# Expert weights through one ring of 22 converted pieces, converted at planned slots, with the staging tiles at another place

## The chip, the cores and the metric

The kernel runs on one core of a Trainium2 chip. The metric is the device time of one execution in microseconds (us). TensorE is called PE, VectorE DVE, ScalarE ACT, GpSimd POOL and SyncE SP. SP issues the DMAs that this text is about.

## The reference

Three layers follow each other: attention with a mask by cluster, a mixture of experts with one expert per token, and a dense layer with a piecewise quadratic activation. The change lies in the second one, which is

```python
for e in range(E):                      # E = 8 experts, N = 1536 tokens, D = 512, F = 1024
    mask = e_idx == e
    h = np.maximum(x[mask] @ w1[e], 0.0)            # w1[e]: 512 x 1024, float32
    ye = h @ w2[e]                                  # w2[e]: 1024 x 512, float32
    out[mask] = gate_w[mask, None] * eom[mask, e, None] * ye
```

All weights of the eight experts are read once: 64 pieces of 512 KB.

## The kernel before, in words

Attention ends with the routing: POOL scatters the tokens' rows (`pay`) to `xs` in DRAM, sorted by expert (L646), and `order()` writes to `regs` which expert comes first, second and so on, largest first. The capacities of the eight places are `CAPS` = 304 to 144 tokens.

Then comes the expert stage, written out by hand slot by slot. A slot is either `l1(r, fc)`, 12 matmuls that make 128 rows of the hidden layer of expert r (hi and lo float16 halves of weights and tokens: L1088, L1089, L1092), or `l2(r, dc)`, 24 matmuls that make 128 rows of its output (L1104 to L1106). After a first stretch of eight `l1` of expert 0, phase r has 12 slots: four `l2` of expert r and eight `l1` of expert r + 1. PE's results go to PSUM (a ring of 7 banks, `ps`) and leave it through ACT (`hT` hi half, L1094) and DVE (`hT` lo half, L1095), or for `l2` through DVE and ACT (L1111 to L1114). `Pipe` emits these steps one slot later. "Urgent" ones come first in a step.

The weights arrive as float32 by SP's DMAs into six staging tiles (`stg`), and each piece is converted into two float16 halves: the hi half by ACT (L1010), the lo half by DVE (L1011); every fourth piece takes two ACT steps (L1006, L1007) and POOL (L1008) instead. The halves go to `wp`, where a whole expert's w1 (`w1h`, `w1l`) and w2 (`w2h`, `w2l`) are tiles with two buffers each. A piece's conversion is emitted one slot after its load (`lag`), all loads of phase r being, one per slot, the four of w2 of expert r + 1 and then the four of w1 of expert r + 2. The instructions of an engine run in the order in which they are emitted, so a conversion that waits for its DMA holds what was emitted behind it on ACT and DVE. `tokens(r, row)` is a transposing DMA from `xs`, also on SP. A load can start when its staging tile was released by the lo half of the piece six before.

In the first slots of each phase from phase 1 on, `windows()` and `ids()` do small steps on DVE and POOL (`ids` scatters the token numbers, L764). `fetch` and `convert` bring the first weights of the dense layer (`w_in`, L1025, L1033 to L1041) at the end of the expert stage. The dense layer (L1265 and on) starts when the experts are done.

Of the kernel before, what the change touches and what calls it, by code (L numbers as in the profile page):

```python
# [7 lines left out]
F32 = mybir.dt.float32  # L8
# [20 lines left out]
CAPS = (304, 256, 224, 208, 192, 176, 176, 144)  # L29
NWIN = 20  # L30
# [110 lines left out]
def build(tc, q, k, v, centroids, w_gate, w_og, w1, w2, w_in, w_out, out):  # L141
# [860 lines left out]
    n_lo, lag = [0], [1]  # L1002
# [9 lines left out]

    def piece(dst_h, dst_l, src, scale):

        a, b = dst_h.shape[1], dst_h.shape[2]
        t = stg.tile([128, a, b], F32, tag="st", name="stg")
        n_lo[0] += 1
        nc.sync.dma_start(out=t, in_=src)
        pool = n_lo[0] > 4 and n_lo[0] % 8 in (1, 5)
        pipe.add(lag[0], lambda: halves(dst_h, dst_l, t, scale, pool))  # L1020
# [30 lines left out]
    def w1_pieces(r, e):  # L1051
        W[r, 1] = t = [wp.tile([128, KD, F], F16, tag=n, name=n) for n in ("w1h", "w1l")]
        return [lambda f=slice(n * 256, (n + 1) * 256): piece(
            t[0][:, :, f], t[1][:, :, f], w1f[ds(e * DM, DM), f].rearrange("(k p) f -> p k f", p=128), SW1) for n in range(4)]

    def w2_pieces(r, e):
        W[r, 2] = t = [wp.tile([128, KF, DM], F16, tag=n, name=n) for n in ("w2h", "w2l")]
        return [lambda n=n: piece(
            t[0][:, 2 * n:2 * n + 2, :], t[1][:, 2 * n:2 * n + 2, :],
            w2f[ds(e * F + n * 256, 256), :].rearrange("(k p) d -> p k d", p=128), SW2) for n in range(4)]  # L1060
# [18 lines left out]
    def l1(r, fc):  # L1079
# [3 lines left out]
        wh, wl = W[r, 1]  # L1083
        p = ps.tile([128, 512], F32, tag="p", name="hps")
        f = slice(fc * 128, (fc + 1) * 128)
# [11 lines left out]
    def l2(r, dc):  # L1097
        cap, c0 = CAP[r], C0[r]
        wh, wl = W[r, 2]
        p = ps.tile([128, 512], F32, tag="p", name="yps")  # L1100
        d = slice(dc * 128, (dc + 1) * 128)
        h = HT[r]
        for f in range(KF):
            nc.tensor.matmul(out=p[:, 0:cap], lhsT=wh[:, f, d], rhs=h[:, 0, f, :], start=(f == 0), stop=False)  # L1104
            nc.tensor.matmul(out=p[:, 0:cap], lhsT=wh[:, f, d], rhs=h[:, 1, f, :], start=False, stop=False)  # L1105
            nc.tensor.matmul(out=p[:, 0:cap], lhsT=wl[:, f, d], rhs=h[:, 0, f, :], start=False, stop=(f == KF - 1))  # L1106
# [10 lines left out]
    PAT = {0: (0, 1, 3, 5)}  # L1117
# [3 lines left out]
    def expert(r):  # L1121
        if r < E:
            eid[r] = reg(regs[0:1, 0, r:r + 1], [ET.SP], E - 1)
# [37 lines left out]
    expert(0), expert(1)  # L1161
    for n, f in enumerate(w1_pieces(0, eid[0])):
        f()
        pipe.step()
        if n == 1:
            tokens(0, row(0))
    ld_q = w2_pieces(0, eid[0]) + w1_pieces(1, eid[1])
    lag[0] = 3
    for n in range(8):
        ld_q[n]()  # L1170
        if n == 1:
            tokens(1, row(1))
        l1(0, n)
        pipe.step()
    gates(0)
    lag[0] = 1
    wnd, idg = windows(), ids()
    for r in range(E):
        expert(r + 2)
        C0[r] = reg(regs[0:1, 2, r:r + 1], ACTDVE, NTK)  # L1180
        ld_q = (w2_pieces(r + 1, eid[r + 1]) if r + 1 < E else []) + (w1_pieces(r + 2, eid[r + 2]) if r + 2 < E else [])
        if r + 3 == E:
            ld_q += [fetch, fetch, fetch]
        if r + 2 == E:
            ld_q += [convert, lambda: None, lambda: None, lambda: None, convert]
        if r + 1 == E:
            ld_q += [convert]
        a, b = 0, 0
        if r + 1 == E:
            pipe.flush()  # L1190
            for _ in wnd:
                pass
            nw = nc.values_load(nwin[0:1, 0:1], min_val=0, max_val=NWIN, skip_runtime_bounds_check_because="a count of windows")
        if 0 in PAT.get(r, ()):
            pipe.step()
        for n in range(12 if r + 1 < E else KD):
            if ld_q:
                ld_q.pop(0)()
            if n == 2 and r + 2 < E:
                tokens(r + 2, row(r + 2))  # L1200
            if n in PAT.get(r, (2, 5, 8, 11)) or r + 1 == E:
                if b < KD:
                    l2(r, b)
                b += 1
            else:
                l1(r + 1, a)
                a += 1
            if r:
                next(wnd, None)
                if n % 3 == 0:  # L1210
                    next(idg, None)
            pipe.step()
        if r + 1 < E:
            gates(r + 1)
        for f in ld_q:
            f()
            pipe.step()
# [5 lines left out]
    with tc.If(nw > 0):  # L1223
        with tc.For_i(0, nw, 1) as i:
            e = reg(tabs[0:1, 0, ds(i, 1)], [ET.SP], E - 1)
            for f in w1_pieces("w", e) + w2_pieces("w", e):
                f()
                pipe.step()
# [132 lines left out]
```

## Time and profile before

| | us |
|---|---|
| median of three executions | 696.34 |
| the three executions | 688.11, 696.34, 697.7 |
| the profiled execution | 688.69 |
| its span in the profile | 686.9 |
| expert stage, first matmul to last | 271.65 to 429.1 |
| dense layer, first matmul | 432.03 |

The span runs from the first to the last instruction, and 1.8 us of the profiled execution lie around it. The executions lie in two groups, one near 688 (the profiled one is among them) and one near 697. Times in rows count from the start of the span.

### The profile page before, as it was taken

How to read it: one execution, taken by the hardware profiler on the slowest of the kernel's cores; microseconds unless marked ns; L12 is line 12 of the kernel's file. 1: busy time of each engine (PE TensorE's matmuls, PEld its weight loads, DVE VectorE, ACT ScalarE, POOL GpSimd, SP SyncE). 2: the span in 40 equal slices, each digit the busy share in tenths (PEclk: the TensorE clock that was granted, in tenths of full speed). 3: DMA queues.
4: the chain of work that ended last, by engine and by line, in shares of the span. 5: the costliest groups of instructions: out<-in, count | busy, mean ns of one | idle time of the engine just before them, and what ended most of it. 6: DMA issues, size and time to landing. Idle time of an engine off the chain costs nothing. (4 is left out here: it accounts for less than half of the span.)

```text
span 686.9 us, 14212 instructions
## 1 busy us (share of the span) xinstructions
PE 594.0 (86%) x5574; PEld 382.1 (56%) x5574; DVE 453.2 (66%) x881; ACT 379.8 (55%) x605; POOL 323.3 (47%) x274
## 2 busy tenths in 40 slices
PE   1798679797979741999989898899999999999996
PEld 1365546565656541689979897344444444444442
DVE  6898978998897962577667768778877874000000
ACT  5387568796869811886667764366657653010000
POOL 9268547786576831234344312276657653021101
PEclk9999878998999955999999999999999999999998
DMA  8877889549732527999999992323322232011000
GB/s 211 171 169 159 179 215 215 134 92 161 143 107 57 89 64 219 323 321 221 183 236 238 286 331 65 113 72 94 106 79 91 92 99 85 1 63 45 24 24 31
DMA packets 142172, 96.30 MB, mean 140 GB/s; under 512 B 97168, under 2 KB 127888, under 8 KB 142096
## 3 DMA queue, kind: packets, MB, share of 16 engines
q1 hardware_dynamic: 139744, 88.60, 52.6%
q0 software_dynamic: 2352, 6.70, 2.7%
q8 instruction: 47, 0.77, 0.5%
q14 instruction: 29, 0.24, 0.1%
HBM read 59.84 MB, written 12.29 MB: 105 GB/s over the span
## 5 line engine op out<-in xcount | busy, mean ns | idle before, releaser
L486 POOL TENSOR_TENSOR pl<-p,ph 128x768 f16<-128x768 f32 x64 | 114.0, 1800 | 47.2 <-ACT ph L480 24.9
L445 DVE TENSOR_REDUCE mq<-s 128x1 f32<-128x768 f32 x96 | 90.5, 950 | 17.8 <-PE s L440 17.5
L475 ACT ACTIVATE p<-st 128x768 f32<-128x768 f32 x96 | 75.8, 810 | 32.6 <-PE st L471 29.5
L480 ACT ACTIVATE ph<-p 128x768 f16<-128x768 f32 x96 | 77.5, 847 | 0.8
L1280 POOL TENSOR_TENSOR gt<-gx,gt 128x512 f16<-128x512 f32 x48 | 55.6, 1159 | 46.7 <-ACT gt L1279 46.7
L1265 PE MATMUL mps<-x,wih 128*128 128x512 f16 x192 | 72.8, 379 | 2.9 <-PEq L1223 2.9
L508 PE MATMUL pv<-vh,pl 128*128 128x65 f16 x576 | 65.9, 200 | 10.4 <-DVE pl L486 10.3
L1088 PE MATMUL hps<-xt,w1h 128*128 128x176 f16 (+6 forms) x256 | 54.0, 264 | 21.9 <-DMA xt<-xs 16.9
L1290 PE MATMUL ops<-woh,gt 128*128 128x512 f16 x192 | 72.8, 379 | 0.0
L1291 PE MATMUL ops<-wol,gt 128*128 128x512 f16 x192 | 72.8, 379 | 0.0
L1292 PE MATMUL ops<-woh,gt 128*128 128x512 f16 x192 | 72.8, 379 | 0.0
L1266 PE MATMUL mps<-x,wih 128*128 128x512 f16 x192 | 72.8, 379 | 0.0
L1267 PE MATMUL mps<-x,wil 128*128 128x512 f16 x192 | 72.8, 379 | 0.0
L470 PE MATMUL st<-aT 128*128 128x384 f16 x192 | 67.1, 350 | 3.9 <-DVE mq L445 2.6
L471 PE MATMUL st<-q2T,bT 82*128 82x384 f16 x192 | 67.1, 349 | 0.6 <-DMA q2T<-kq 0.6
L506 PE MATMUL pv<-vh,ph 128*128 128x65 f16 x576 | 66.6, 200 | 0.0
L507 PE MATMUL pv<-vl,ph 128*128 128x64 f16 x576 | 66.3, 198 | 0.0
L1104 PE MATMUL yps<-hT,w2h 128*128 128x176 f16 (+6 forms) x256 | 63.3, 254 | 2.7 <-DVE hT L1095 2.1
L1105 PE MATMUL yps<-hT,w2h 128*128 128x176 f16 (+6 forms) x256 | 63.3, 254 | 0.4 <-DVE hT L1095 0.2
L1106 PE MATMUL yps<-hT,w2l 128*128 128x176 f16 (+6 forms) x256 | 63.3, 254 | 0.0
L440 PE MATMUL s<-bT 80*128 80x384 f16 x192 | 51.6, 367 | 13.0 <-ACT p L475 5.6
L1274 ACT ACTIVATE sq<-cl,c 128x512 f32<-128x512 f32 x48 | 34.6, 722 | 50.2 <-DVE cl L1272 49.6
(220 smaller groups left out, 1435.9 us busy)
## 6 DMA issues: line engine op xcount, KB each, us to landing
stg<-in_moe_w_dram SPq DMA_DIRECT2D x64, 512.0 KB, 6.8
stg<-in_moe_w_in_dram SPq DMA_DIRECT2D x16, 512.0 KB, 3.6
stg<-in_moe_w_out_dram SPq DMA_DIRECT2D x16, 512.0 KB, 3.6
xs<-zrow SPq DMA_DIRECT2D x16, 288.0 KB, 3.8
kqf<-in_k_dram SPq DMA_DIRECT2D x16, 192.0 KB, 3.3
kqf<-in_q_dram SPq DMA_DIRECT2D x16, 192.0 KB, 3.3
vf<-in_v_dram SPq DMA_DIRECT2D x16, 192.0 KB, 3.4
xs<-zrow SPq DMA_DIRECT2D x8, 108.0 KB, 3.7
```

The source lines that it names most:

```text
L445: nc.vector.tensor_reduce(out=mq[:, i, t:t + 1], in_=lg_t.pop((i, t))[:, :, 0:HS], axis=AX.XY, op=ALU.max)
L470: nc.tensor.matmul(out=o, lhsT=aT[i][:, c, 0, :], rhs=aT[i][:, ts, 1, :], start=True, stop=False)
L471: nc.tensor.matmul(out=o, lhsT=bT[i][0:KS2, 0, c, :], rhs=q2T[i][0:KS2, ts, :], start=False, stop=True)
L475: nc.scalar.activation(out=p.rearrange("p (e s) -> p e s", e=2), in_=lg_t.pop(("t", i, c))[:, :, 0:HS], func=AF.Exp, scale=SCALE)
L480: nc.scalar.activation(out=ph_t[i, c], in_=p_t[i, c], func=AF.Copy)
L486: eng.tensor_tensor(out=pl_t[i, c], in0=p_t.pop((i, c)), in1=ph_t[i, c], op=ALU.subtract)
L1265: nc.tensor.matmul(out=p, lhsT=wih[:, kk, :], rhs=x2[:, 0, kk, c], start=(kk == 0), stop=False)
L1266: nc.tensor.matmul(out=p, lhsT=wih[:, kk, :], rhs=x2[:, 1, kk, c], start=False, stop=False)
L1267: nc.tensor.matmul(out=p, lhsT=wil[:, kk, :], rhs=x2[:, 0, kk, c], start=False, stop=(kk == KD - 1))
L1290: nc.tensor.matmul(out=p, lhsT=gt[:, 0, f, c], rhs=woh[:, f, :], start=(f == 0), stop=False)
L1291: nc.tensor.matmul(out=p, lhsT=gt[:, 0, f, c], rhs=wol[:, f, :], start=False, stop=False)
L1292: nc.tensor.matmul(out=p, lhsT=gt[:, 1, f, c], rhs=woh[:, f, :], start=False, stop=(f == KF2 - 1))
```

## The change

Converted weights are no longer held as whole experts. Each piece of 128 x 4 x 256 elements gets its own pair of tiles (`wh`, `wl`) from one ring of 22 (`NWP`), used in the order in which PE needs the pieces. A piece of w2 is now half of the hidden rows and half of the output columns, so an `l2` needs two pieces instead of four, and a row of such a load is 1 KB instead of 2 KB. The slots are listed first (`slots`), with the same patterns as before. A plan (`when`) says ahead of which slot each piece is converted: from an assumed time of arrival (1.75 us a piece, 2.75 us for a transposing DMA, `come`) and an assumed time of each slot (`at`). A load is issued right behind the conversion of the piece six before it. The conversion's ACT steps are now emitted at once, ahead of that slot's matmuls and of the eviction steps of the slot before; the lo half still comes through `Pipe` one step later. `tokens(r + 2)` moves to the first slot of phase r; the three `fetch` move to the middle of phase 5, ahead of the last five weight loads (before, of the last four); the `convert` steps move to slots 6 and 10 of phase 6 and to the first slot of phase 7; `nw` is read one phase earlier. The pools are opened in another order, so that `stg` and `wp` lie behind `hp`, `yp`, `wn` and `xp` in SBUF, over other tiles of the attention.

```diff
-    stg = mes.enter_context(tc.tile_pool(name="stg", bufs=6))
-    wn = mes.enter_context(tc.tile_pool(name="wn", bufs=1))
-    wp = mes.enter_context(tc.tile_pool(name="wp", bufs=2))
-    xp_ = mes.enter_context(tc.tile_pool(name="xp", bufs=2))
     hp = mes.enter_context(tc.tile_pool(name="hp", bufs=2))
     yp = mes.enter_context(tc.tile_pool(name="yp", bufs=3))
+    wn = mes.enter_context(tc.tile_pool(name="wn", bufs=1))
+    xp_ = mes.enter_context(tc.tile_pool(name="xp", bufs=2))
+    stg = mes.enter_context(tc.tile_pool(name="stg", bufs=6))
+    wp = mes.enter_context(tc.tile_pool(name="wp", bufs=NWP))
...
-        pipe.add(lag[0], lambda: halves(dst_h, dst_l, t, scale, pool))
...
+    def load(r, e, z, j):
+
+        t = stg.tile([128, KD, 256], F32, tag="st", name="stg")
+        f, d = j % 2, j // 2
+        src = w1f[ds(e * DM, DM), j * 256:(j + 1) * 256] if z == 1 else w2f[ds(e * F + f * 512, 512), d * 256:(d + 1) * 256]
+        nc.sync.dma_start(out=t, in_=src.rearrange("(k p) f -> p k f", p=128))
+        staged.append((r, z, j, t))
+
+    def conv():
+        r, z, j, t = staged.pop(0)
+        n_lo[0] += 1
+        W[r, z, j] = h, l = [wp.tile([128, KD, 256], F16, tag=n, name=n) for n in ("wh", "wl")]
+        halves(h, l, t, SW1 if z == 1 else SW2, n_lo[0] > 4 and n_lo[0] % 8 in (1, 5))
...
+    when, come = {}, -5.0
+    for k, p in enumerate(pieces):
+        come += 1.75 + (2.75 if p[1:] == (1, 0) else 0.0)
+        n = 0
+        while n < use[p] - 2 and (at[n] < come + 0.5 or k >= NWP and n <= rel[pieces[k - NWP]]):
+            n += 1
+        when.setdefault(n, []).append(p)
...
+    NST = 6
+    for k in range(NST):
+        next_load()
+        if k == 1:
+            tokens(0, row(0))
...
+        for _ in when.get(n, ()):
+            conv()
+            next_load()
+            if n == 0:
+                pipe.step()
+        if first and ph + 2 < E:
+            tokens(ph + 2, row(ph + 2))
+        if (ph, m) == (E - 3, 6):
+            for _ in range(3):
+                fetch()
+        if (ph, m) in conv64:
+            convert()
+        (l1 if z == 1 else l2)(r, i)
```

The order on SP at the start of the expert stage, before. `DMASW` semaphores are those of the scatters to `xs`:

```order
L1046 TENSOR_LOAD regs [waits DVE_49]
L1046 TENSOR_LOAD regs
L1018 ISA
L1018 DMA stg<-in_moe_w_dram 128x4x256 [waits DMASW6_49,DMASW7_49,DMASW5_49,DMAHW0_49,DMASW4_49,DMAHW1_49,DMASW3_49,DMAHW2_49,DMASW2_49,DMAHW3_49,DMASW1_49,DMAHW4_49,DMASW0_49,DMAHW5_49,DVE_49,DMAHW6_49,PE_49,DMAHW7_49,Activation_49,Pool_49]
L1018 ISA
L1018 DMA stg<-in_moe_w_dram 128x4x256
L1046 TENSOR_LOAD regs
L1065 ISA
L1065 DMA_TRANSPOSE xt<-xs 128x4x304
```

The same place after:

```order
L1038 TENSOR_LOAD regs [waits DVE_49]
L1050 ISA
L1050 DMA stg<-in_moe_w_dram 128x4x256 [waits DMAHW2_49,DMAHW3_49,DMAHW1_49,DMAHW4_49,DMAHW0_49,DMAHW5_49,DVE_49,DMAHW6_49,PE_49,DMAHW7_49,Activation_49,Pool_49]
L1050 ISA
L1050 DMA stg<-in_moe_w_dram 128x4x256 [waits DMAHW4_49]
L1038 TENSOR_LOAD regs
L1062 ISA
L1062 DMA_TRANSPOSE xt<-xs 128x4x304 [waits DMAHW5_49,DMASW7_49,DMASW3_49]
L1063 ISA
```

The wait for the scatters moved from the first weight load to the first transposing DMA; the two loads stand ahead of it as before.

The order on ACT around the change from expert 6 to expert 7 and up to the last weights, before (the first `hT` of 128x144 is the first result of expert 7, and `w2h` are the last four pieces):

```order
L1046 TENSOR_LOAD regs
L1094 ACTIVATE hT<-hps 128x144
L1006 ACTIVATE stg<-stg 128x1024
L1007 ACTIVATE w2h<-stg 128x1024
L1113 ISA
L1113 ACTIVATE x_5482<-yps 128x176
L1094 ACTIVATE hT<-hps 128x144
L1010 ACTIVATE w2h<-stg 128x1024 x2
L1094 ACTIVATE hT<-hps 128x144
L1010 ACTIVATE w2h<-stg 128x1024
```

The same place after, from the fourth `hT` of expert 7 on (L1032 and L1033 belong to `convert`; two pieces of expert 7's w2 follow later still, in phase 7):

```order
L1091 ACTIVATE hT<-hps 128x144
L1011 ACTIVATE wh<-stg 128x1024 x2
L1091 ACTIVATE hT<-hps 128x144
L1032 ACTIVATE wih<-cw 128x512
L1033 ACTIVATE cv<-cw 128x512
L1110 ISA
L1110 ACTIVATE x_5482<-yps 128x176
L1091 ACTIVATE hT<-hps 128x144
L1007 ACTIVATE stg<-stg 128x1024
L1008 ACTIVATE wh<-stg 128x1024
L1011 ACTIVATE wh<-stg 128x1024
```

Before, the four conversions of expert 7's w2 stand behind its first, second and third `hT`; after, the first of them (L1007, L1008) stands behind the sixth `hT` of that expert.

## Rows read from the trace of the kernel before

**Rows 1.** The page: span, busy time of each engine, share, instructions.

```profile
span 686.9 us, 14212 instructions
PE 594.0 (86%) x5574; PEld 382.1 (56%) x5574; DVE 453.2 (66%) x881; ACT 379.8 (55%) x605; POOL 323.3 (47%) x274
```

**Rows 2.** PE's timeline: start, length, instruction, idle time before, what ended it.

```profile
271.65 0.41 PE L1088 MATMUL hps<-xt,w1h 128*128 128x304 f16 x1 [16.91 <-DMA xt<-xs]
...
428.89 0.23 PE L1106 MATMUL yps<-hT,w2l 128*128 128x144 f16 x1
432.03 0.38 PE L1265 MATMUL mps<-x,wih 128*128 128x512 f16 x1 [2.92 <-PEq L1223]
```

**Rows 3.** Waits of PE from 262 to 436: total, times, longest.

```profile
PE hps L1088 <- DMA xt<-xs: 16.9, 1, 16.9
PE hps L1088 <- DVE hT L1095: 5.0, 3, 2.2
...
PE yps L1104 <- DVE hT L1095: 2.1, 3, 1.1
PE gp L1074 <- DVE hT L1095: 1.6, 1, 1.6
PE yps L1104 <- ACT hT L1094: 0.6, 1, 0.6
```

**Rows 4.** Stretches of 24 matmuls: length, busy times, PE's clock, DMA share, GB/s.

```profile
352.36:355.76 3.40, 3.40 (x25) 3.17 (x25) 3.40 (x9) 2.38 (x7) 0.00 (x0) 0.56 1.52 137
357.90:359.88 1.98, 1.98 (x27) 1.98 (x26) 1.92 (x4) 1.91 (x3) 1.82 (x2) 1.00 1.08 309
410.88:412.39 1.51, 1.51 (x27) 1.51 (x25) 0.92 (x4) 1.51 (x4) 1.40 (x1) 1.00 0.05 20
416.54:419.28 2.74, 2.74 (x24) 2.63 (x24) 2.74 (x4) 1.04 (x3) 1.16 (x1) 0.54 0.63 185
```

**Rows 5.** ACT's timeline at two conversions that waited for their piece.

```profile
349.01 1.06 ACT L1010 ACTIVATE w1h<-stg 128x1024 f16<-128x1024 f32 x1 [3.48 <-DMA stg<-in_moe_w_dram]
408.71 1.06 ACT L1006 ACTIVATE stg<-stg 128x1024 f32<-128x1024 f32 x1 [3.45 <-DMA stg<-in_moe_w_dram]
```

**Rows 6.** DVE's timeline at the same two places.

```profile
350.33 0.37 DVE L1095 SCALAR_TENSOR_TENSOR hT<-hps,hT 128x208 f16<-128x208 f32 x1 [4.35 <-ACT hT L1094]
350.62 1.21 DVE L1011 SCALAR_TENSOR_TENSOR w1l<-stg,w1h 128x1024 f16<-128x1024 f32 x1
...
411.28 0.31 DVE L1095 SCALAR_TENSOR_TENSOR hT<-hps,hT 128x144 f16<-128x144 f32 x1 [4.63 <-ACT hT L1094]
```

**Rows 7.** Waits of SP from 262 to 436.

```profile
SPq L1018 <- DVE w2l L1011: 17.5, 12, 3.2
SPq L1018 <- POOL w1l L1008: 12.5, 7, 2.5
...
SPq L1018 <- DMA xs<-pay,pos: 3.8, 1, 3.8
```

**Rows 8.** SP's timeline: the first weight loads and the first transposing DMA.

```profile
264.83 1.02 SPq L1018 DMA_DIRECT2D stg<-in_moe_w_dram  x2
266.31 1.82 SPq L1065 DMA_TRANSPOSE xt<-xs  x1
```

**Rows 9.** Line L1018: the last load's start, and from its start to its landing.

```profile
L1018 SPq DMA_DIRECT2D stg<-in_moe_w_dram x1: 372/372/372, 402.5 to 402.5; - x1
...
DMA to landing us min/median/max: 10.1/10.1/10.1
```

**Rows 10.** Stretches as in Rows 4, for the last two columns, DMA share and GB/s.

```profile
310.20:312.20 2.00, 2.00 (x21) 1.61 (x19) 1.89 (x5) 0.75 (x2) 0.00 (x0) 1.00 0.02 5
396.00:405.00 9.00, 9.00 (x123) 8.77 (x121) 7.65 (x12) 7.32 (x16) 2.13 (x1) 1.00 1.09 348
406.00:410.00 4.00, 4.00 (x60) 4.00 (x58) 0.65 (x3) 1.25 (x2) 0.00 (x0) 1.00 1.05 385
324.00:332.00 8.00, 8.00 (x78) 7.22 (x77) 5.68 (x9) 3.64 (x9) 3.91 (x3) 1.00 0.98 154
```

More of the change, by code (lines that the diff above doesn't have):

```diff
@@ L1115, in l2 @@
         pipe.add(1, scaled, True)
-    PAT = {0: (0, 1, 3, 5)}
+    PAT = {0: (0, 1, 3, 5), E - 1: range(KD)}
+    slots = [(1, 0, n, -1) for n in range(KF)]
+    for r in range(E):
+        a = b = 0
+        for n in range(KF + KD if r + 1 < E else KD):
+            if n in PAT.get(r, (2, 5, 8, 11)):
+                slots.append((2, r, b, r))
+                b += 1
+            else:
+                slots.append((1, r + 1, a, r))
+                a += 1
+    at, use, rel = [0.0], {}, {}
+    for n, (z, r, i, _) in enumerate(slots):
+        for j in ([i // 2] if z == 1 else [i // 2 * 2, i // 2 * 2 + 1]):
+            use.setdefault((r, z, j), n)
+            rel[r, z, j] = n
+        at.append(at[-1] + (12 if z == 1 else 24) * CAPS[r] / 2400)
+    pieces = sorted(use, key=lambda k: use[k])
+    when, come = {}, -5.0
[5 more added lines that the diff above has]
+        when.setdefault(n, []).append(p)
     ACTDVE = [ET.Activation, ET.DVE]
@@ L1159, in row @@
         return reg(regs[0:1, 1, r:r + 1], [ET.SP], (E - 1) * NTK)
-    expert(0), expert(1)
-    for n, f in enumerate(w1_pieces(0, eid[0])):
-        f()
-        pipe.step()
[L1165 to L1217, printed above, removed]
@@ new lines, in build, with next_load @@
+    left = list(pieces)
+    def next_load():
+        if left:
+            r, z, j = left.pop(0)
+            if r not in eid:
+                expert(r)
+            load(r, eid[r], z, j)
+    NST = 6
[3 more added lines that the diff above has]
+            tokens(0, row(0))
+    wnd, idg = windows(), ids()
+    phase = -2
+    conv64 = [(E - 2, 6), (E - 2, 10), (E - 1, 0)]
+    for n, (z, r, i, ph) in enumerate(slots):
+        first = ph != phase
+        if first:
+            phase, m = ph, 0
+            if z == 2:
+                pipe.step()
+            if ph >= 0:
+                C0[ph] = reg(regs[0:1, 2, ph:ph + 1], ACTDVE, NTK)
+            if ph == E - 2:
+                nw = nc.values_load(nwin[0:1, 0:1], min_val=0, max_val=NWIN, skip_runtime_bounds_check_because="a count of windows")
+        for _ in when.get(n, ()):
+            conv()
+            next_load()
+            if n == 0:
+                pipe.step()
+        if first and ph + 2 < E:
[6 more added lines that the diff above has]
+        (l1 if z == 1 else l2)(r, i)
+        if z == 1 and i + 1 == KF:
+            gates(r)
+        if ph >= 1:
+            next(wnd, None)
+            if m % 3 == 0:
+                next(idg, None)
+        m += 1
+        pipe.step()
@@ L1225, in build @@
             e = reg(tabs[0:1, 0, ds(i, 1)], [ET.SP], E - 1)
[L1226 to L1228 removed]
+            for z in (1, 2):
+                for j in range(4):
+                    load("w", e, z, j)
+                    pipe.step()
+                    conv()
+                    pipe.step()
             tokens("w", reg(tabs[0:1, 1, ds(i, 1)], [ET.SP], E * NTK - 128))
```

33 lines of the change are left out of this document (10 added, 23 removed).

## The prediction

> **What bounds the kernel now.** The page says that PE is busy for 594.0 of 686.9 us [rows 1]. The dense layer behind the experts runs PE without a break, so a gain has to come from the time up to its first matmul at 432.03. The expert stage takes from 271.65 to 429.1 on PE (the last row's start and length) [rows 2]; the gap of 2.92 behind it is a branch, which stays. I read next what PE waits for in it [rows 3]: first 16.9 us for the first tokens, which is the change of stage; then 8.7 us (5.0 + 2.1 + 1.6) for DVE's `hT`, the step that empties PSUM. DVE is not the cause: its `hT` at 350.33 and 411.28 waited 4.35 and 4.63 for ACT [rows 6], and ACT stood before a conversion whose piece had not landed, 3.48 and 3.45 us [rows 5]. The second one is a piece of w2 of expert 7, which PE first uses in the last phase, some 14 us later (four `l2` of 1.51 [rows 4] ahead of 429.1). So PE is held not by weights that it needs, but by evictions that are queued behind a conversion of weights that it does not need yet. Two of these pauses cost a second time: behind them PE's clock was granted at 0.56 and 0.54 on the mean of the stretch, between the levels of 1.2 and 2.4 GHz, and the same 24 matmuls took 3.40 instead of 1.98 and 2.74 instead of 1.51 [rows 4], together 2.65 us.
>
> The transfers are the second bound, close to the first. The last weight load starts at 402.5 and lands 10.1 later, at 412.6 [rows 9]; DMA engines were idle for two clear us around 311, and in the other stretches of those rows their share is near or over 1 [rows 10].
>
> **The start.** SP's wait of 3.8 us ahead of the first weight load is for the scatters, which read `pay` [rows 7]; the staging tile lay over it. After the change the first load waits for no scatter, and the transposing DMA waits for them, which it has to for its data. The first two loads thus move from 264.83 to about 261.0, and the transposing DMA, now not behind them, from 266.31 [rows 8] to about 264.3 (264.83 less 0.5 for the ten semaphores that SP stepped through). PE starts when it lands. If it takes the same time from its issue, that is 2.0 us; at most the two loads (1.4 us each by the rates below) no longer move ahead of it either, with half of this hidden by its own issue of 1.82: 3.4. Against it, the last scatters now share the DMA engines with two loads; a scatter of 0.29 MB would at most take 0.9 longer (its own time again at 348 GB/s), so that the gain lies between 1.1 and 3.4. I take 2.5, near the upper middle, since the two loads need 2.8 us and have 3.3 of their own ahead of 264.3. The Trainium skill (DMA: Bandwidth & Descriptors, Queues, rings and completion order) says that an engine takes turns between the queues that have work, packet by packet; by it the 0.9 would be paid in full and the term be 1.6. No row here shows two such queues beside each other.
>
> **PE's waits.** A conversion now stands at the slot for which its piece is planned to have landed, and w2 pieces of expert 7 stand behind the sixth `hT` of that expert and later, where before the first stood behind its first `hT`. If pieces land on time, the 8.7 us of waits and the 2.65 of clock go: 11.3. What stays are 0.6 for ACT's `hT` right behind the first expert's `l1` [rows 3], as the slots there are the same, the small pause between slots, and the lower clock at the start. PE alone would then end at 429.1 - 11.3 - 2.5 = 415.3.
>
> **The transfers.** The number of loads, transposing DMAs and `ids` scatters is unchanged. Three things move the last landing: the start, -3.8; the idle time at 311, where SP stood before `tokens`, -2.0 if nothing new idles; and the rows of w2, which halve to 1 KB. Between 396 and 405 w1 and `w_in` moved, 1 KB rows, at 348 GB/s; from 406 to 410 w2, 2 KB rows, at 385 [rows 10]. A piece of 0.524 MB takes 1.51 instead of 1.36 us, over 32 pieces of w2 4.6 us more. The last landing is then 412.6 - 3.8 - 2.0 + 4.6 = 411.4. Behind it come its hi half, 1.06 [rows 5], its lo half, 1.21 [rows 6], the rest of the `l2` that needs it from its middle on, 0.75, and one more `l2`, 1.51 [rows 4], and 0.2 to the end: 416.1. So the transfers would end the stage 0.8 later than PE alone. The slow stretch around 324 to 332 (154 GB/s at a share of 0.98 [rows 10], some 4.5 us lost) is in both kernels. The Trainium skill's rule speaks otherwise here: its table of DMA properties (DMA: Bandwidth & Descriptors, Specifications) puts the smallest transfer for full rate at 512 B, so 1 KB rows would cost nothing and the transfers end at 411.5; the two rates above disagree with it, and the sum goes by the rates.
>
> **Other steps.** ACT, DVE and POOL convert as many elements as before (64 pieces, 15 of them with POOL), and PE's matmuls are the same, so these cost nothing as long as they lie in the evictions' gaps. The conversion's ACT steps now come ahead of the eviction of the slot before, which delays that eviction by 1.06 or 2.1 us; seven PSUM banks cover this, and without them it would be paid at each of the 64. The `convert` steps stay in phase 6 and 7; three DVE steps of 0.7 us each sit beside evictions there, as they did before, and are part of the waits around 416. Reading `nw` earlier only moves a register load. A ring of 22 pieces against 16 gives no wait of its own: the tile that a conversion takes over was last read more than two experts earlier. New waits can come where transposing DMAs, slow stretches and `w_in` fall together with a conversion. Bounds: none, or the 11.3 us of before again. The three old blocks (around 350, 388 and 416) cost 3.8 each; I allow half a block, 1.9, since most conversions are planned several slots ahead of their piece's use, but the transfers have hardly any reserve.
>
> **The sum.** The later of 415.3 and 416.1, plus 1.9, is 418.0, 11.1 earlier than before. The profiled execution took 688.69, so that the same execution would take 677.6. The median of before lies 7.65 above that execution, as two of three lie in a group near 697. What makes the groups I do not know, and a median of three can fall into either, so I add half of it, 3.8: 681.4 us. The 2% that a measurement of this kernel can tell from no change are 13.9 us.
>
> **Rivals.**
> First, everything goes: no new wait, and 1 KB rows as fast as 2 KB. PE alone sets the end, 415.3, and the profiled execution would take 674.9. For it speaks that the conversions are the only thing seen in the way of evictions; against it the two rates. 0.2.
> Second, it doesn't do what it says: the loads stay the bound. A load still waits for the lo half of the piece six before it; SP stood 17.5 and 12.5 us in such waits [rows 7]. Now the conversion is tied to a slot, so a load may be held by PE's progress, where before it followed the landing. If DMA engines idle for 6 us in all by this (a tenth of a us per piece), the end moves to 424, the gain is 5, and the execution takes 683.6. 0.2.
> Third, slower: pieces land later than the plan says (10.1 us from start to landing for the last one [rows 9]), and as the conversion is now emitted ahead of evictions at every slot, each late piece holds ACT. With one block of 3.8 in each of eight phases, 30.4 us come and 13.0 (429.1 to 416.1) go: 706.1. It decides from the seventh block on, where 26.6 reaches 13.0 + 13.9. 0.1, since on the average the plan's rate (eight pieces of 1.75 and 2.75, 16.8 us a phase) is near what the rates give: 12.1 for eight pieces, and a transposing DMA and a share of the slow stretches on top.
>
> **How the numbers follow.** The forecast has 0.5. The low end is the first rival with the better start (674.0), with 2 to 3 us of scatter: 671. The high end is the second rival in the upper group (691.3) with the worse start and some scatter: 694; it leaves out the third rival and little else. Faster by over 2% comes from two thirds of the first rival (0.13), two fifths of the forecast (0.20) and a little of the second (0.02); slower from most of the third (0.08); the rest is within.
>
> **What would show it.** In the changed kernel's profile: first weight load near 261 and first matmul near 269; PE's waits for `hT` in the expert stage under 3 us in all; the clock at 1.00 from soon behind the first matmuls to the end; the last landing near 411; the first matmul of the dense layer near 421. Wrong would be: ACT waiting over 3 us for a piece at several slots, PE's clock at half in the middle of the stage, a share of the DMA engines under 0.5 for several us, or w2 loads at 385 GB/s in spite of their short rows.

## The result and the profile after

The changed kernel takes 701.16 us (median of 20 executions, 695.59 to 706.27) against 694.61 of the kernel before (20 executions): ratio 1.0118, 95% interval 1.0087 to 1.0149. The ratio compares the faster executions of the two kernels, so it is not the quotient of the two medians, which is 1.0094. By the ratio the changed kernel is 8 us slower (6 to 10), within the 2% that count as no change; 681.4 was forecast, and the range ended at 694.

The profiled execution took 703.38, more than the median; the one of the kernel before, 688.69, lies near the low end of its executions (688.11 to 701.40). The two profiles are thus 14.7 us apart, almost twice what the times say, and part of that is scatter. Its page:

```profile
span 701.6 us, 14199 instructions
PE 605.0 (86%) x5574; PEld 385.8 (55%) x5574; DVE 456.0 (65%) x881; ACT 380.3 (54%) x605; POOL 322.1 (46%) x274
```

PE's timeline at the first matmul of the experts, the last one and the first of the dense layer, which answer to [rows 2]:

```profile
273.53 0.41 PE L1085 MATMUL hps<-xt,wh 128*128 128x304 f16 x1 [15.27 <-DVE wl L1012]
...
442.02 0.23 PE L1103 MATMUL yps<-hT,wl 128*128 128x144 f16 x1
444.61 0.38 PE L1282 MATMUL mps<-x,wih 128*128 128x512 f16 x1 [2.36 <-PEq L1237]
```

From the first of them to the third it is 171.08 us; before it was 160.38. So the expert stage is 10.7 of the 14.7 us longer; 1.9 come ahead of it and 2.1 behind it. What comes ahead is not the change: the routing's last step, which everything waits for, is DVE's `CAST` to `regs`, and it came at 257.99 before and at 261.59 here (over all profiles of this text, whose code up to there is the same, it came between 258 and 267):

```profile
261.59 0.17 DVE L687 CAST regs<-rf 1x32 int32<-1x32 f32 x1
```

From its end to PE's first matmul it was 13.5 us before and is 11.8 now. What follows is the stage. PE's waits from 262 to 448, the answer to [rows 3]:

```profile
PE hps L1085 <- DVE wl L1012: 15.3, 1, 15.3
PE hps L1085 <- DMA xt<-xs: 7.6, 2, 4.5
PE yps L1103 <- DVE wl L1012: 4.5, 4, 1.5
PE hps L1086 <- DVE wl L1012: 4.0, 4, 2.0
...
PE yps L1102 <- DVE hT L1092: 1.1, 1, 1.1
PE yps L1101 <- DVE hT L1092: 0.5, 1, 0.5
```

The 15.3 are the change of stage. Of the waits for `hT`, 9.3 in [rows 3], 1.6 are left. In their place stand two that before did not have: 8.5 us in eight waits for a lo half `wl` that DVE has not made yet, and 7.6 in two waits for the tokens of experts 4 and 5. Behind them the clock falls. Stretches of PE alone: length, busy time, clock, DMA share, GB/s:

```profile
359.94:366.77 6.83, 5.03 (x32) 0.50 0.99 297
383.83:387.25 3.42, 3.12 (x22) 0.50 0.90 252
288.26:291.67 3.41, 3.41 (x16) 0.50 0.91 284
sum 13.66, PE 11.55; mean PE 3.85
```

At 0.50 the granted clock is 1.2 GHz, so of 11.55 busy us half, 5.8, is lost by estimate; the first two stretches follow the waits for tokens, the third a wait of 2.0 for `wl`. Together this is 8.5 + 7.6 + 1.6 + 5.8 = 23.5 us, against 9.3 + 2.65 = 11.95 before: 11.5 more, for a stage that grew by 10.7.

The transfers, in stretches with all engines (the last three columns are clock, DMA share and GB/s):

```profile
292.00:296.00 4.00, 3.44 (x26) 2.15 (x24) 1.99 (x3) 2.95 (x6) 0.00 (x0) 1.00 0.04 12
...
369.00:376.00 7.00, 7.00 (x85) 7.00 (x83) 4.09 (x9) 5.57 (x10) 3.69 (x2) 1.00 0.97 45
...
412.00:427.00 15.00, 13.66 (x186) 12.80 (x183) 12.11 (x24) 11.85 (x25) 4.28 (x3) 1.00 1.10 348
```

Three things are to be seen. Weights still move at 348 GB/s in a clear stretch. DMA engines are idle at 292, because SP stands before loads whose staging tile is not free (one wait of 7.0 for a lo half between 287 and 298). Over the stage its waits for lo halves are now 57.9 us:

```profile
SPq L1050 <- DVE wl L1012: 44.3, 22, 7.0
...
SPq L1050 <- POOL wl L1009: 13.6, 10, 2.3
```

Before they were 42.6: the 17.5 and 12.5 of [rows 7], 0.6, and a row that [rows 7] leaves out:

```profile
SPq L1018 <- POOL w2l L1008: 12.0, 6, 4.5
```

And at 369 the engines are busy to 0.97 and move 45 GB/s. In such stretches `ids` scatters are in flight, twelve issued between 311.5 and 375, 8.8 us from issue to landing in the median. The tokens of expert 4 were issued into such a stretch (349 to 353, 59 GB/s), and PE waited for them:

```profile
348.66 6.87 SPq L1065 DMA_TRANSPOSE xt<-xs  x1
```

```profile
361.74 0.32 PE L1085 MATMUL hps<-xt,wh 128*128 128x192 f16 x1 [4.55 <-DMA xt<-xs]
```

They took 12.9 us from issue to landing; the median of such transfers was 6.9 before. They also had less time: they were issued 13.1 us ahead of PE's first use, before 21 (331.31 to 352.36), although they now stand in the first slot of the phase.

### The profile page after: what moved, and what is told of

Same layout as the page of the kernel before. It is cut to its first block, busy times and chain, and to the rows that moved or that the text cites. A ratio compares the mean times of both kernels' runs of the same rounds, so it can differ in the third digit from the quotient of the medians.

```text
span 701.6 us, 14199 instructions
## 1 busy us (share of the span) xinstructions
PE 605.0 (86%) x5574; PEld 385.8 (55%) x5574; DVE 456.0 (65%) x881; ACT 380.3 (54%) x605; POOL 322.1 (46%) x274
## 5 line engine op out<-in xcount | busy, mean ns | idle before, releaser
L1009 POOL TENSOR_TENSOR wl<-stg,wh 128x1024 f16<-128x1024 f32 x15 | 33.2, 2214 | 108.8 <-ACT wh L1008 108.8
L1085 PE MATMUL hps<-xt,wh 128*128 128x176 f16 (+6 forms) x256 | 55.4, 268 | 22.9 <-DVE wl L1012 15.3
L471 PE MATMUL st<-aT 128*128 128x384 f16 x192 | 69.9, 364 | 2.5 <-DVE mq L446 1.5
L472 PE MATMUL st<-q2T,bT 82*128 82x384 f16 x192 | 70.2, 366 | 0.8 <-DMA q2T<-kq 0.8
L1012 DVE SCALAR_TENSOR_TENSOR wl<-stg,wh 128x1024 f16<-128x1024 f32 x49 | 65.3, 1344 | 7.9 <-ACT wh L1011 7.9
L507 PE MATMUL pv<-vh,ph 128*128 128x65 f16 x576 | 68.7, 203 | 0.0
L508 PE MATMUL pv<-vl,ph 128*128 128x64 f16 x576 | 68.3, 201 | 0.0
L1011 ACT ACTIVATE wh<-stg 128x1024 f16<-128x1024 f32 x49 | 51.2, 1057 | 31.0 <-DMA stg<-in_moe_w_dram 30.7
L1103 PE MATMUL yps<-hT,wl 128*128 128x176 f16 (+6 forms) x256 | 63.4, 255 | 4.7 <-DVE wl L1012 4.5
L1102 PE MATMUL yps<-hT,wh 128*128 128x176 f16 (+6 forms) x256 | 63.4, 254 | 1.1 <-DVE hT L1092 1.1
```

The lines of the kernel that those rows point to most:

```text
L471: nc.tensor.matmul(out=o, lhsT=aT[i][:, c, 0, :], rhs=aT[i][:, ts, 1, :], start=True, stop=False)
L472: nc.tensor.matmul(out=o, lhsT=bT[i][0:KS2, 0, c, :], rhs=q2T[i][0:KS2, ts, :], start=False, stop=True)
```

## Experiments

The theories, as the traces suggested them. In the first four runs the first is that tokens come late by their place in SP's queue, the second that six staging tiles hold the loads. Later runs name them A (the 1 KB rows of w2), B (the `ids` scatters' slow stretches), C (loads held by conversions that come late) and D (PE itself waits for lo halves of pieces that have long landed). "Stage" is the time from the first matmul of the experts to the first of the dense layer in the profiled execution; it was 160.4 before and 171.1 after. Ratios are to the kernel before, timed on the same chip, from four to ten executions of each run. A stage is one execution and scatters by some us: with the staging tiles moved the kernel before has 165.0 and is faster all the same. So differences of under 5 us in that column say little.

| run | us | ratio, 95% interval | stage |
|---|---|---|---|
| tokens first | 708.63 | 1.0125, 0.9991 to 1.0259 | 176.0 |
| tokens a phase earlier | 706.27 | 1.0216, 1.0139 to 1.0293 | 174.6 |
| nine staging tiles | 706.33 | 1.0137, 1.0050 to 1.0224 | 170.7 |
| before, staging tiles moved | 694.79 | 0.9936, 0.9880 to 0.9993 | 165.0 |
| before, scatters later | 687.30 | 0.9876, 0.9792 to 0.9960 | 153.9 |
| before, both of these | 686.19 | 0.9853, 0.9807 to 0.9899 | 152.2 |
| before, 1 KB rows | 698.98 | 1.0058, 1.0019 to 1.0097 | 168.0 |
| before, 1 KB rows, scatters later | 686.03 | 0.9877, 0.9773 to 0.9981 | 155.7 |
| after, 2 KB rows | 715.48 | 1.0278, 1.0165 to 1.0391 | 186.6 |
| after, 2 KB rows, scatters later | 703.49 | 1.0114, 1.0010 to 1.0219 | 173.5 |
| after, scatters later | 693.80 | 0.9929, 0.9887 to 0.9972 | 160.6 |
| ... and nine staging tiles | 693.00 | 0.9967, 0.9925 to 1.0010 | 159.1 |
| ... and four slots | 685.99 | 0.9882, 0.9845 to 0.9918 | 155.8 |
| ... and the plan 4 us earlier | 682.81 | 0.9807, 0.9705 to 0.9910 | 149.7 |
| ... and four slots, plan 4 us earlier | 679.82 | 0.9804, 0.9734 to 0.9874 | 152.0 |
| ... and four slots, plan 8 us earlier | 686.10 | 0.9905, 0.9863 to 0.9946 | 155.1 |
| after, four slots | 704.84 | 1.0109, 0.9978 to 1.0240 | 169.2 |
| after, four slots, plan 4 us earlier | 699.59 | 1.0060, 1.0010 to 1.0111 | 171.5 |

**Tokens ahead of the first slot's loads**, in the changed kernel:

```diff
+        if first and ph >= 0 and ph + 2 < E:
+            tokens(ph + 2, row(ph + 2))
         for _ in when.get(n, ()):
             conv()
             next_load()
...
-        if first and ph + 2 < E:
+        if first and ph < 0:
             tokens(ph + 2, row(ph + 2))
```

> The changed kernel, with tokens(r + 2) ahead of the first slot's loads on SP instead of behind them. Theory 1 (the loss is SP's queue: a load that waits for the lo half of the piece six before holds the transposing DMA behind it, and PE waits for late tokens): the two long waits for tokens (7.6 us in all) and the clock behind them go, 8 to 12 us faster than the changed kernel, ratio to the kernel before near 0.998. Theory 2 (the loads are held by the slots of the conversions, DMA engines idle, everything lands late): the waits move from the tokens to the weights, within 4 us of the changed kernel, ratio 1.006 to 1.012.

Measured 1.0125, not the 0.998 of the first theory. The waits moved; PE's, from 272 on (the 16.8 are 15.0 for the change of stage and 1.8):

```profile
PE hps L1085 <- DMA xt<-xs: 16.8, 2, 15.0
PE yps L1103 <- DVE wl L1012: 5.5, 5, 2.0
PE yps L1101 <- ACT hT L1091: 4.2, 1, 4.2
PE hps L1086 <- DVE wl L1012: 4.0, 4, 2.0
PE yps L1101 <- ACT g L1073: 2.5, 1, 2.5
```

**Tokens a whole phase earlier**, into a third tile (the ring has 20 pieces to make room):

```diff
-        if first and ph + 2 < E:
-            tokens(ph + 2, row(ph + 2))
+        if first and ph < 0:
+            tokens(1, row(1))
+        if (ph, m) == (-1, 4):
+            tokens(2, row(2))
+        if first and 0 <= ph < E - 3:
+            tokens(ph + 3, row(ph + 3))
```

> The changed kernel with each expert's tokens issued a whole phase earlier, into a third tile (the ring has 20 pieces for it, which moves no conversion). Theory B in its narrow form (the tokens are late because their DMA is issued late and meets the scatters): the pauses at slots 44 and 56 go, 8 to 10 us, ratio 0.998 to 1.003. If what is short is the transfers' time itself: PE waits for weights at other slots instead, as when the tokens went ahead of one slot's loads, 1.007 to 1.015.

Measured 1.0216, above both forecasts and no better than the changed kernel. No wait for tokens is left, and PE waits for evictions instead:

```profile
PE yps L1103 <- DVE wl L1012: 5.0, 5, 1.4
PE hps L1086 <- DVE wl L1012: 4.0, 4, 2.0
PE yps L1102 <- DVE hT L1092: 3.6, 3, 2.0
PE hps L1085 <- DVE hT L1092: 3.0, 3, 1.6
PE yps L1101 <- ACT g L1073: 2.7, 1, 2.7
```

The place of the tokens alone is thus not the cause: whoever goes first, somebody waits while the scatters run. The first theory falls.

**Nine staging tiles** instead of six, the ring at 20 pieces:

```diff
-NWP = 22
+NWP = 20
-    stg = mes.enter_context(tc.tile_pool(name="stg", bufs=6))
+    stg = mes.enter_context(tc.tile_pool(name="stg", bufs=9))
-    NST = 6
+    NST = 9
```

> The changed kernel with nine staging tiles instead of six, so that a load is issued behind the conversion of the piece nine before (the ring of converted pieces is 20 for the space; the plan is the same with it). Theory 2 (loads are held by the conversions' slots): DMA engines no longer idle between the first two transposing DMAs, and the stage gains 6 to 12 us, ratio 0.995 to 1.003. Theory 1 (SP's queue ahead of the tokens): loads ahead of the tokens wait for the same lo halves, under 3 us, ratio 1.007 to 1.012.

Measured 1.0137: nothing gained. PE still waits 4.6 + 3.9 for `wl` and 9.0 ahead of experts 4 and 5.

**The staging tiles alone**, in the kernel before (`stg` and `wp` behind `hp`, `yp`, `wn` and `xp` in the order of the pools):

```diff
+    hp = mes.enter_context(tc.tile_pool(name="hp", bufs=2))
+    yp = mes.enter_context(tc.tile_pool(name="yp", bufs=3))
+    wn = mes.enter_context(tc.tile_pool(name="wn", bufs=1))
+    xp_ = mes.enter_context(tc.tile_pool(name="xp", bufs=2))
     stg = mes.enter_context(tc.tile_pool(name="stg", bufs=6))
-    wn = mes.enter_context(tc.tile_pool(name="wn", bufs=1))
     wp = mes.enter_context(tc.tile_pool(name="wp", bufs=2))
...
```

> The kernel before, with nothing but the pools opened in the changed kernel's order. If the place of the staging tiles gives the earlier start that was forecast: the first weight load stands about 2.5 us behind regs and not behind the scatters, first matmul 1.5 to 3 us sooner after regs, ratio 0.996 to 0.998. If the loads from the new place are slower or the start is given back by later waits: 1.000 or more.

Measured 0.9936, 4.4 us (0.5 to 8.3). From `regs` to the first matmul it took 11.0 us instead of 13.5. The rest of the 4.4 is in no row: in the profile the stage behind it is longer than before.

**The scatters later**, in the kernel before: `ids` steps in the first half of the dense layer.

```diff
-                if n % 3 == 0:
-                    next(idg, None)
...
-    for _ in idg:
-        pass
...
             if (fc, g) in slots64:
                 convert()
+            next(idg, None)
             pipe.step()
+    for _ in idg:
+        pass
```

> The kernel before, with the scatters of the token numbers (ids, L764) moved from the expert stage into the dense layer. If they make the slow stretches of the transfers (154 GB/s at a share of 0.98 from 324 to 332): these go, DMA has some 10 us less to do, and PE's waits for hT shrink by 3 to 8 us, ratio 0.989 to 0.996. If the stretches have another cause: no change, ratio 0.998 to 1.002.

Measured 0.9876, 8.6 us (3 to 14). From 310 to 400 the transfers move 238 GB/s with the scatters and 269 without (the last columns are clock, DMA share, GB/s):

```profile
310.00:400.00 90.00, 84.46 (x930) 81.45 (x929) 64.76 (x129) 63.37 (x109) 36.23 (x22) 0.98 1.07 238
```

```profile
310.00:400.00 90.00, 89.79 (x980) 85.68 (x979) 71.08 (x137) 69.58 (x119) 21.50 (x10) 1.00 0.87 269
```

The same move in the **changed kernel**:

> The changed kernel with the ids scatters moved behind the expert stage, into the first half of the dense layer. In the kernel before the same move gave 0.9876. Theory A and theory C: it gains what it gave there, 8 to 9 us, and stays about 12 us above the kernel before with the same move, 692 to 694 (ratio 0.995 to 1.0). Theory B: the pauses for tokens of 4.8 and 3.3 us with their half clock (some 12 us) go as well, and the time comes to 680 to 684 (ratio 0.98 to 0.985), level with or below the kernel before with the same move.

Measured 0.9929, about the time that A and C gave. It gains 13 us where the kernel before gains 8.6, but the two intervals are too wide to tell these gains apart, or the two kernels, between which 0.5% remain. No wait for tokens is left within the stage, as B said, although they were issued only 10.6 and 9.4 us ahead of experts 4 and 5; they landed after 6.7 in the median. The waits for `wl` stay at 8.4. So B holds for the tokens, and something else is left.

**The rows of w2.** In the changed kernel, 2 KB rows again; an expert's first `l2` then needs all four pieces:

```diff
+            nc.sync.dma_start(out=t.rearrange("p (a k) f -> p a (k f)", a=2), in_=w2f[ds(e * F + j * 256, 256), :].rearrange("(k p) d -> p k d", p=128))
...
-        for j in ([i // 2] if z == 1 else [i // 2 * 2, i // 2 * 2 + 1]):
+        for j in ([i // 2] if z == 1 else range(4)):
```

> The changed kernel with w2 loaded again in rows of 2 KB, 256 rows by 512 columns a piece, as before; an expert's first l2 then needs all four pieces, as before. Theory A (the rows): the 1 KB rows of w2 are what costs. By the packets of the expert stage, 34,700 of 1 KB at a mean of 61 ns after against 18,900 at 54 and 8,200 of 2 KB at 111 before, they take 11.7 us more of the 16 DMA engines, and the transfers set the end, so the time falls by 8 to 12 us to about 691 (ratio to the kernel before 0.99 to 1.0). Theory B (the ids scatters' slow stretches meet tokens that have no reserve): the time stays within 3 us of the changed kernel's, 698 to 704. Theory C (a load is held until PE has come to the slot of its conversion): also 698 to 704, and the idle stretches of the DMA engines stay.

The same with the scatters later:

> The changed kernel with both: w2 in rows of 2 KB and the ids scatters behind the expert stage. Theory A with the scatters' own price: about 682 (ratio 0.98). If both A and B hold, 674 to 678 (0.97 to 0.976), below the kernel before with the scatters moved. Theory C: 692 to 694, no more than the scatters' own price.

Measured 1.0278 and 1.0114, slower by 1.6 and 1.9% than the same with 1 KB rows. This does not price the rows, since the order of need changed with them; PE's waits up to 445 in the first of the two say so (8.5 in the changed kernel):

```profile
PE hps L1087 <- DVE wl L1012: 13.0, 7, 4.2
PE yps L1104 <- DVE wl L1012: 9.3, 7, 3.1
```

The clean form is the other way round, 1 KB rows in the **kernel before**, with its order kept:

```diff
-            t[0][:, 2 * n:2 * n + 2, :], t[1][:, 2 * n:2 * n + 2, :],
-            w2f[ds(e * F + n * 256, 256), :].rearrange("(k p) d -> p k d", p=128), SW2) for n in range(4)]
+            t[0][:, n % 2 * KD:n % 2 * KD + KD, n // 2 * 256:n // 2 * 256 + 256],
+            t[1][:, n % 2 * KD:n % 2 * KD + KD, n // 2 * 256:n // 2 * 256 + 256],
+            w2f[ds(e * F + n % 2 * 512, 512), n // 2 * 256:n // 2 * 256 + 256].rearrange("(k p) d -> p k d", p=128), SW2) for n in range(4)]
```

> The kernel before with nothing changed but the shape of a w2 piece: 512 rows by 256 columns, rows of 1 KB, as in the changed kernel. Theory A: slower by 5 to 12 us than the kernel before (ratio 1.007 to 1.017), since its loads are close to the bound, and the 1 KB packets of the expert stage come to over 55 ns on the mean with a total of 6 to 12 us more on the 16 DMA engines. Theories B and C: within 0.5% of the kernel before; by the prediction's own rates 4.6 us more of transfers, of which up to 4 would show.

And with the scatters later as well:

> The kernel before with w2 in rows of 1 KB (alone 1.0058) and the ids scatters behind the expert stage (alone 0.9876). If the rows cost by themselves: 0.992 to 0.995. If they cost only because transfers have no reserve while the scatters run: 0.986 to 0.99, level with the scatters moved alone.

Measured 1.0058, 4.0 us (1.3 to 6.7), and 0.9877 against 0.9876 with 2 KB rows: nothing. The same 90 us of the two runs, first with the scatters, then without:

```profile
310.00:400.00 90.00, 82.73 (x834) 78.39 (x833) 58.23 (x117) 57.39 (x96) 37.60 (x22) 0.94 1.05 220
```

```profile
310.00:400.00 90.00, 90.00 (x999) 86.67 (x997) 70.71 (x136) 69.36 (x119) 22.32 (x11) 1.00 0.87 260
```

With the scatters the engines are full at 220 GB/s, and the old order too has waits for `hT` of 3.9 + 3.1 + 0.3 there; without them they have time to spare at 260, and PE waits for nothing. With 2 KB rows the same stretch gave 238 and 269. So in this stretch the rows can cost time only where the scatters leave no reserve. The two times alone would not show it: each of their intervals is about 1% to either side, more than the price of the rows.

**Four slots of lead** instead of two, in the changed kernel, which moves 16 conversions at the start and the end:

```diff
-        while n < use[p] - 2 and (at[n] < come + 0.5 or k >= NWP and n <= rel[pieces[k - NWP]]):
+        while n < use[p] - 4 and (at[n] < come + 0.5 or k >= NWP and n <= rel[pieces[k - NWP]]):
```

> The changed kernel, where a conversion stands at the latest four slots ahead of its piece's first use instead of two; it moves 15 of the 64 conversions, at the start (slots 0 to 11) and the end (79 to 92). Theory D (two slots are too few: the hi half on ACT, the lo half a step later behind evictions on DVE; at the end pieces lie landed for 10 us before their lo half is made): the pauses for wl at slots 5 to 9 (5.7 us) and 83 to 95 (7.5) shrink to what the kernel before had there (1.7 and 6.0) or less, the time falls by 4 to 8 us, to 693 to 697 (ratio 1.0 to 1.006). Theory A (the 1 KB rows set the end) and theory B (the scatters): the pauses only move, within 2 us of the changed kernel (1.009 to 1.014).

Measured 1.0109, not to be told from the changed kernel: what D forecast did not come. With the **scatters later**, and then with the **plan 4 us earlier** as well:

```diff
-    when, come = {}, -5.0
+    when, come = {}, -9.0
```

> The same with the ids scatters behind the expert stage; without the four slots this gave 0.9929. Theory D: 4 to 8 us less, 0.981 to 0.987, below the kernel before with the scatters moved (0.9876). Theories A and B: 0.99 to 0.995.

> The run before this with the plan's arrivals 4 us earlier as well (its clock starts at -9 instead of -5), so that conversions in the middle stand some three slots earlier. Theory C (loads are held since a staging tile comes free only at the slot of the conversion): the idle stretches of the DMA engines up to 360 shrink, and 2 to 4 us more go, 0.977 to 0.984. Theory D alone: nothing more, or 1 to 3 us back, since ACT waits for pieces and evictions stand behind it, 0.983 to 0.99.

Measured 0.9882, between the forecasts, and 0.9804, in the range of C; this second interval lies wholly below that of the changed kernel with the scatters later. Another 4 us gives nothing more:

> The fastest run so far (four slots, scatters moved, plan's arrivals 4 us earlier: 0.9804) with the arrivals another 4 us earlier (-13). Theory C: the idle stretches of the DMA engines shrink again, 0.975 to 0.98. Theory D alone: the conversions now stand ahead of the landing, ACT waits for pieces, PE for evictions, 0.982 to 0.99.

Measured 0.9905, and not less than the run before, whose interval just reaches into this one. Conversions then stand ahead of their landing, and PE waits 5.5 us for `hT` (2.5 + 1.7 + 1.3; 3.7 in the run before), none for `wl`.

**Which side of a late conversion costs.** With the scatters later, nine staging tiles relieve the loads alone; the plan 4 us earlier, at two slots, moves 61 of the 64 conversions, by three slots most of them, and the loads that stand behind them:

> The changed kernel with the ids scatters moved (0.9929) and nine staging tiles instead of six, the ring at 20 pieces for it, which moves no conversion. Theory C (held loads): the DMA engines' idle stretch around 292 to 300 goes, and with it 4 to 8 us, 0.982 to 0.988. Theory D (PE waits for lo halves at the start and the end): the waits for wl stay as they are and the time too, 0.99 to 0.995.

> The changed kernel with the ids scatters moved and the plan's arrivals 4 us earlier (-9), with two slots of lead as they are, so that what moves is mostly the conversions in the middle, three slots. Theory C: 4 to 6 us less than 0.9929, so 0.984 to 0.987. Theory D: the same, 0.99 to 0.995; the four slots are then what made the earlier plan pay.

Measured 0.9967 and 0.9807. PE's waits for `wl` with nine tiles:

```profile
PE yps L1103 <- DVE wl L1012: 4.6, 4, 1.5
PE hps L1086 <- DVE wl L1012: 4.0, 4, 2.0
```

and with the earlier plan:

```profile
PE hps L1086 <- DVE wl L1012: 0.8, 1, 0.8
```

The last weight loads, with nine tiles and with the earlier plan:

```profile
L1050 SPq DMA_DIRECT2D stg<-in_moe_w_dram x3: 373/382/491, 395.5 to 400.0; - x3
```

```profile
L1050 SPq DMA_DIRECT2D stg<-in_moe_w_dram x4: 373/724/1753, 397.5 to 403.7; - x4
```

From PE's first matmul (270.69 and 275.08) to the last load it is 129 us in both, 137 in the changed kernel with the scatters later. So both relieve the loads alike, as far as the last one tells, and only the one that also moves the conversions gains (the two intervals do not meet): held loads (C) are not the bound, late conversions (D) are. D's own forecast for the earlier plan missed, as it took that plan to move the middle only; it moves the start and the end too, where these waits lie. What a late conversion is shows at the end of the stage in the changed kernel with the scatters later, where no transfer disturbs. The last two loads and their time to landing:

```profile
L1050 SPq DMA_DIRECT2D stg<-in_moe_w_dram x2: 373/373/373, 408.8 to 410.0; - x2
...
DMA to landing us min/median/max: 6.6/6.8/6.9
```

DVE's two lo halves of them, and PE:

```profile
423.27 3.31 DVE L1012 SCALAR_TENSOR_TENSOR wl<-stg,wh 128x1024 f16<-128x1024 f32 x2
```

```profile
426.64 0.24 PE L1103 MATMUL yps<-hT,wl 128*128 128x144 f16 x1 [1.18 <-DVE wl L1012]
```

The last piece landed at 416.9 (410.0 + 6.9); its lo half was made at 426.6. It lay for almost 10 us, since its conversion stands at slot 92, its lo half a step behind that, and on DVE behind evictions and `convert`.

**With the scatters where they were**, four slots and the earlier plan give less:

> The changed kernel with the conversions four slots ahead at the latest and the plan's arrivals 4 us earlier; the ids scatters stay in the expert stage. Theory C (conversions that come late hold the loads, and this is what leaves the tokens no reserve): most of what the earlier plan gave without scatters comes here too, 5 to 8 us, and the pauses at slots 44 and 56 halve: ratio 0.998 to 1.005. Theory B (the scatters alone make these pauses): they stay, 1.005 to 1.011.

Measured 1.0060, 4 us below the changed kernel's 1.0118, but the intervals overlap, and in the profile the stage is no shorter (171.5): the time is in B's range. Waits for `wl` fall to 1.2, and PE waits for evictions and gates behind late pieces, as before the change:

```profile
PE yps L1101 <- DVE hT L1092: 6.2, 2, 4.5
PE yps L1101 <- ACT g L1073: 4.0, 1, 4.0
PE hps L1085 <- DMA xt<-xs: 3.9, 2, 2.8
```

**The kernel before with the two cheap parts**, staging tiles moved and scatters later:

> The kernel before with two things alone: the staging tiles where the changed kernel has them (alone 0.9936), and the ids scatters behind the expert stage (alone 0.9876). If the two add up: 0.979 to 0.983, which puts it level with the best form of the ring; if both gain at the same wait for transfers, 0.985 to 0.99.

Measured 0.9853, in the second range; its interval holds the sum too (0.981), so whether the gains add up is not shown. The ring with the scatters later, four slots and the earlier plan, 0.9804, is the fastest form run, 679.82 us, faster than both kernels; it is not told from this one, since the intervals overlap.

## Why the prediction was wrong

**What bounds the kernel** was read rightly. Evictions behind conversions held PE, and when conversions were tied to the plan's slots, the waits for `hT` fell from 9.3 to 1.6, as forecast (under 3). What took their place was not.

**The start** was right. 2.5 was forecast; the two profiled executions give 1.7 from `regs` to the first matmul, the staging tiles alone 2.5. Over all profiles it is 13.9 on average in the four with the old place of the tiles and 11.4 in the sixteen with the new one: 2.4. The first load came at 265.7 and not near 261; of these 4.7 us, 3.6 are the routing, which ended later in that execution. The Trainium skill (DMA: Bandwidth & Descriptors, Queues, rings and completion order) says that an engine takes turns between the queues that have work; the 1.6 that was worked out with it lies further from the runs than 2.5, and whether the engines took turns no run shows.

**The rows** were sized rightly as far as the runs tell, 4.6 forecast and 4.0 measured (1.3 to 6.7), but the price has a condition that I did not see: from 310 to 400 it shows in PE's waits only while the scatters fill the engines, and without them it is hidden (no wait of PE over 0.2 us there with either rows). The sentence that the slow stretch "is in both kernels" covered this up; it is in both, but with short rows the transfers of these 90 us come to less (220 against 238 GB/s). The rule of the Trainium skill (DMA: Bandwidth & Descriptors, Specifications) that rows from 512 B on move at full rate would have put the term at nothing; 348 GB/s at 412 to 427 of the changed kernel against 385 in [rows 10] still speaks against it.

**New waits** is the step that failed: "I allow half a block, 1.9, since most conversions are planned several slots ahead of their piece's use". The condition is wrong where it counts. All eight waits for lo halves lie at the start and the end (282 to 296 and 420 to 440), where the plan's limit of two slots decides for most pieces, as their planned arrival is later still. What came instead of 1.9 were 8.5 us in waits for lo halves, with 1.7 lost to the clock behind one of them, and 7.6 for tokens, with 4.1 lost to the clock. The stage, forecast at 152 us (269 to 421), took 171. The tokens' part goes with the scatters, but these are in the kernel before too, without such a wait; there the tokens had 21 us, here 13, and what took the difference was not singled out. The first part is shown to come from the plan, with the scatters later: moving it by 4 us took the waits from 8.4 to 0.8 and the time from 0.9929 to 0.9807, 8.5 us (the intervals of the two just overlap; those of the run with four slots as well, 0.9804, do not). I looked only for conversions that stand too early, with ACT waiting for a piece, and not for ones that stand too late, with PE waiting for a piece that has landed.

**The transfers** failed with it. The last landing was forecast near 411; the last load starts at 423.3, and DMA engines stay full until 430 (3.6 of these 19 us are the later routing). The sum let nothing hold a load behind a slot; that was left to the second rival, at 6 us. And the chain from the last landing to its lo half, 2.27 in the sum, was almost 10 where it can be read (the scatters later).

**The sum and the budget.** By single prices, the staging tiles give -0.64%, the rows +0.58%; if prices add, what is left of +1.18% is 1.24%, 8.6 us, to about 5 either way by the three intervals. The plan 4 us earlier is worth 1.22% with the scatters out of the way, but with them, and with four slots, only 0.6%, not clear of the noise. What the loss is with the scatters in place is thus shown only in part. Whether the other half lies in the order of transfers beside the scatters or in a better plan for that case stays open; a plan fitted to the scatters was not tried. The 3.8 us for two groups of executions had no ground: twenty executions fill the range from 688 to 701 without a gap, and the routing's end alone moves by almost 9 us.

**The rivals.** The second (loads held by slots) was seen, DMA engines idle at 292 to 300, but nine tiles did not bring it back as time: it was not the bound. Its reading of [rows 7] missed a row of 12.0. The third had the direction; its 17.4 us are twice the 8 measured, and its mechanism is the opposite one. That 706.1 lies near the 703.38 of the profiled execution is luck: it starts from 688.69, one of the shortest executions of the kernel before. (Seven blocks, 26.6, do not quite reach 13.0 + 13.9 either.) Of the signs named beforehand, two decided: the clock at half in the middle of the stage, and the share of the DMA engines under 0.5 for several us. "ACT waiting over 3 us for a piece" was the wrong thing to watch: after 280 it happened once (5.24 at 336).

## What to carry to other kernels

Work that follows a transfer can be placed too early (the engine that does it is held, and all that is queued behind) or too late (the one that needs it is held); when it is moved from one side, the other has to be priced by the same rows, down to the last step of the chain, here a lo half that runs a step later behind evictions. A plan's constants are part of such a change: with the scatters out of the way 4 us on its clock were worth as much as the whole change cost, and 8 us no more than that. Before the order of large transfers is tuned, look for small ones that run beside them: moving twelve scatters out of the stage gave 8.6 us in the kernel before. And one profile is one execution: compare the stages that the change touches, and set their difference beside that of the times.

## What was not expected of the hardware

The `ids` scatters write 4 bytes to a row. With twelve of them in the stage, DMA engines stay busy and move 45 GB/s over 7 us (369 to 376), and 220 instead of 260 GB/s over 90 us (the kernel before with 1 KB rows). The Trainium skill (DMA: Bandwidth & Descriptors, Specifications) says that transfers below 512 B are done by reading and writing back; that this is how they slow the others was not tested, only that over 90 us the rate rises when they go. And a lo half on DVE took 2.6 us beside POOL's lo half, instead of 1.22, at 285.30 of the profile after.

```profile
284.70 2.12 POOL L1009 TENSOR_TENSOR wl<-stg,wh 128x1024 f16<-128x1024 f32 x1 [20.07 <-ACT wh L1008]
```

```profile
285.30 2.60 DVE L1012 SCALAR_TENSOR_TENSOR wl<-stg,wh 128x1024 f16<-128x1024 f32 x1
```
